# Three edits on one core: a stack loaded from GpSimd's queue, a normalisation moved to GpSimd, and a reordered chain of last reciprocals

## The chip, the cores and the metric

The kernel runs on one core of a Trainium2 chip. The metric is device time in microseconds (us), the median of several executions. Engines are named as the profile names them: PE (matrix multiplication; PEld its weight loads), DVE (vector), ACT (scalar, with the activation functions), POOL (GpSimd) and SP, which here only issues DMAs. ACT and POOL issue DMAs too, each into a queue of its own.

## The reference

For x of 2048 tokens by 640 channels the reference returns a gated sum of an attention block (32 heads of width 20) and a token-mixing MLP:

```python
x = A_x
g = _sigmoid((x * gate_w).sum(-1, keepdims=True))
a = _A_ref(x, A_wqkv, A_wo)                  # softmax(q k^T * Dh**-0.5) v, then @ wo
b = _B_ref(x, B_w1, B_b1, B_w2, B_b2)        # layernorm; u = gelu(w1^T h + b1); y = w2^T u + b2
return g * a + (1 - g) * b
```

All inputs are fp32. The kernel splits most operands into a high and a low part (`hi_lo`, lines 39 to 44) and multiplies them in three passes: high by high, high by low, low by high.

## The kernel before

The kernel runs in stages; times are from the profiled execution.

*Projections (0 to 221 us).* `qk_unit` forms q and k, then the v loop forms v; all go to DRAM. In the last 24 qk units (lines 545 to 576, from 137 us) the first half of x's channels is also loaded (`h_load`), normalised (`h_norm`: subtract the mean, multiply by 1/std) and split (`h_split`: ACT makes the high part `hh`, POOL the low part `hl`). From unit 8 on, the first score stack is loaded as well. A *stack* is the operand of one pair of heads, copied together from DRAM: `ks` (k, three times) and two `qs` halves. With `eng=None` its DMAs are not issued at once but put on a list, `drip`, from which the loops issue one or two at a time.

*MLP with the maximum pass (221 to 738 us).* For each half d of the channels there are 14 u tiles (`u`, layer one) and 16 y tiles (`y`, layer two). The weights are loaded by SP (`w_raw`, line 514), some nine pieces ahead, into 8 buffers, and split by ACT (`wh`) and POOL (`wl`). PE's order comes from a generator, `mlp`, and between its steps the loop at line 798 puts *score* steps: a score matmul `s` (line 210) goes to PSUM, and DVE takes row maxima of it (line 216), or, in pairs, of a score plus the part of another that ACT has cut at zero (lines 225 and 235). The maxima `m` go to DRAM; the attention loop's exponential uses them. How many score steps stand by MLP step n is set by `dve_room(n)`: it gives DVE an even load, of 435 ns for a score step and, in the first half's y tiles, 600 ns for each normalisation of the second half. That normalisation is done there, one tile of 128 tokens in each y tile, by DVE for d = 1 and by POOL for d = 0 (line 483). In this stage the order on ACT, DVE, POOL and SP is also that in which the code emits instructions; a small model of time (`clock`, `act`, `later_on`) decides when each is emitted.

At score step 552 the loop asks for the first *exponential* stack (`st_src[0]`: 20 DMAs), its maxima (`load_m`: eight DMAs of one 4 KB row) and `load_v(0)` (one DMA), all on `drip`; one entry is issued per two score steps, behind what is left of the score stack of that time.

*Attention (738 to 1712 us).* 16 pairs of heads, 32 steps each: two score matmuls into PSUM, exponential on ACT, `pv` with v, and the rest of the score steps. Outputs `o` and row sums `l` go to DRAM; reciprocals of the sums are stored to DRAM, spread over the head's rows (`r_d`).

*Output projection (1712 to 1789 us).* For token tiles t = 1 to 15, PE forms `a` tiles from the first 512 rows of o (called e: `ore` times reciprocals `rbe`, loaded two token tiles at a time by `e_load`) and, from t = 8 on, from the last 128 rows (called l: `orl`, `rbl`) as well. Each `a` tile has a pair of PSUM banks; there are two such pairs. The last four heads' sums come late: `last_load` reads them, `last_recip` inverts them on DVE and stores them to `rc_d`, and `l_rest` loads them back into the last 80 rows of `rbl`, once per head row, four DMAs. The other rows of `orl` and `rbl` are loaded by POOL in `l_load`.

Of the kernel before, what the change touches and what calls it, by code (L numbers as in the profile page):

```python
# [10 lines left out]
OP = mybir.AluOpType  # L11
AX = mybir.AxisListType

P = 128
S, D, H, DH, F = 2048, 640, 32, 20, 1728
NP = H // 2
NT = S // P
NC = D // P
FF = 13
FT = 14  # L20
NDIFF = 8
LAST = 4
# [4 lines left out]
NPAIR = VW * 2  # L27
# [4 lines left out]
def gated_mix(ctx, tc, xT, x, wqk, wv0, wv1, wo, w1, w1t, b1, w2, b2, out):  # L32
    nc = tc.nc
# [30 lines left out]
    rc_d = dram.tile([LAST, S], F32, name="rc_d")  # L64
    r_d = dram.tile([H, DH, S], F32, name="r_d")
    v_d = dram.tile([2, NT, P, 16 * VW], F32, name="v_d")
# [30 lines left out]
    def k8(shape, dt, name):  # L97
        return base.tile(shape, dt, tag="k8", bufs=3, name=name)

    def q4(shape, dt, name):  # L100
        return base.tile(shape, dt, tag="q4", bufs=6, name=name)
# [10 lines left out]
    negm = cp.tile([P, NT], F32, name="negm")  # L112
    ssq = cp.tile([P, NT], F32, name="ssq")
    rstd = cp.tile([P, NT], F32, name="rstd")
# [1 line left out]
    omg = cp.tile([P, NT], F32, name="omg")  # L116
    b2o = cp.tile([P, NT], F32, name="b2o")

    drip = []

    def load_stack(p, ks, qs, full, eng=nc.sync):
        put = eng.dma_start if eng else lambda *a: drip.append(lambda: nc.sync.dma_start(*a))
        for j in range(2):
            r0 = 64 * j
            h = 2 * p + j
            rows = slice(DH * h, DH * h + DH)
            kf = ks.bitcast(F32)
            cut = 0 if full or p >= NDIFF else S if j else S // 2
            for n, lo in enumerate((0, 0, 1)):
                r = slice(r0 + n * DH, r0 + (n + 1) * DH)  # L130
                if cut:
                    put(kf[r, :cut], kd_d[lo, rows, :cut])
                if cut < S:
                    put(kf[r, cut:], k_d[lo, rows, cut:])
            if full:
                put(kf[r0 + 3 * DH: r0 + 3 * DH + 2, :], ones)
            for i in range(2):
                qf = qs[i].bitcast(F32)
                cols = slice(i * (S // 2), (i + 1) * (S // 2))
                put(qf[r0: r0 + DH, :], q_d[0, rows, cols])  # L140
                put(qf[r0 + DH: r0 + 2 * DH, :], q_d[1, rows, cols])
                put(qf[r0 + 2 * DH: r0 + 3 * DH, :], q_d[0, rows, cols])

    def base_stack(p, full, eng=nc.sync):
        ks = k8([P, S], F32R, f"ks{p}_{full}")
        qs = [q4([P, S // 2], F32R, f"qs{p}_{full}_{i}") for i in range(2)]
        load_stack(p, ks, qs, full, eng)
        return ks, qs

    def load_m(p, qs, half, put=nc.sync.dma_start):  # L150
        src = m_d[p, half].rearrange("(g i j t) r -> i j t g r", i=2, j=2, t=8)
        for j in range(2):
            for i in range(2):
                r = 64 * j + 3 * DH + i
                dst = qs[half].bitcast(F32)[r: r + 1, :].rearrange("o (t g r) -> o t g r", g=4, r=32)
                put(dst, src[i: i + 1, j])

    s_src, st_src, v_tiles = {}, {}, {}

    def load_v(p):  # L160
        v_tiles[p] = base.tile([P, NT, NPAIR], F32, tag="v", bufs=2, name=f"v{p}")
        c0 = NPAIR * (p % 8)
        nc.sync.dma_start(v_tiles[p], v_d[p // 8, :, :, c0: c0 + NPAIR].rearrange("t p c -> p t c"))

    s_close = []

    def s_max(p, half, parts):
        mm = cp.tile([P, 16], F32, tag="mm", bufs=2, name=f"mm{p}_{half}")
# [14 lines left out]
    def s_next():  # L183
        next(stream)()
        for e in list(s_close):
            e[0] -= 1
            if e[0] <= 0:
                s_close.remove(e)
                e[1]()
# [242 lines left out]
    for half in range(2):  # L432
        wvh, wvl = wvs[half]
        width = HALF + 2 if half == 0 else HALF
        for t in range(NT):
            n = NT * half + t
# [43 lines left out]

    def h_norm(d, t):
        xm = xms[d, t]
        (nc.vector if d else nc.gpsimd).tensor_scalar(xm, xm, negm[:, t:t + 1], rstd[:, t:t + 1], op0=OP.add, op1=OP.mult)  # L483

    def h_split(d, t):
        xm = xms.pop((d, t))
# [18 lines left out]
    def w_raw(k):  # L505
        src, _ = w_list[k]
        n, m = src.shape[1], src.shape[2]
        if k < AHEAD:
            raw = p1.tile([P, 4, P], F32, tag="xr", bufs=2, name=f"wr{k}")
        elif k < 2 * AHEAD:  # L510
            raw = q4([P, 4, P], F32, f"wr{k}")
        else:
            raw = gp.tile([P, 4, P], F32, tag="wr", bufs=8, name=f"wr{k}")
        (nc.scalar if k < 2 * AHEAD else nc.sync).dma_start(raw[:, :n, :m], src)
        w_raws.append(raw)
# [31 lines left out]
    for n, (m, q) in enumerate(units):  # L547
# [26 lines left out]
        if n == 22:  # L574
            w_split(2)
            w_raw(4)
            w_raw(5)
    xps.close()

    gps = ExitStack()  # L580
    gp = gps.enter_context(tc.tile_pool(name="gp", bufs=1, side="right"))
# [21 lines left out]
    def settle(ns):  # L603
        clock[0] += ns
        for e in sorted(e for e in events if e[0] <= clock[0]):
            events.remove(e)
            e[2]()
        while free[0] <= clock[0] + 100:
            e = min((e for e in act_q if e[1] <= clock[0] + 100), default=None)
            if e is None:  # L610
                break
            act_emit(e)
# [151 lines left out]
    S_AHEAD = NDIFF * 128 + 2 + 48  # L764
    STEPS = 2 * ((FT - 1) * 48 + 32 + NT * 40)
# [4 lines left out]

    hooks[0] = start_ahead
    FIRST = 14
    U_STEPS = (FT - 1) * 48 + 32
    DIFF, RAW, NORM = 435, 640, 600

    def dve_work(k):
        return DIFF * min(k, NDIFF * 128) + RAW * max(0, k - NDIFF * 128)

    def dve_room(n):
        norms = min(max((n - U_STEPS) / (NT * 40), 0), 1) * NT * NORM  # L780
        return (dve_work(S_AHEAD) + NT * NORM) * (n + 1 - FIRST) / (STEPS - 20 - FIRST) - norms

    first_p = {}

    def first_scores(n):
        ks, qs = st_src[0]
        ps = psum.tile([P, 2, 512] if n == 0 else [P, 512], F32, tag=("two", "s3", "pv")[n], bufs=1, name=f"stf{n}")
        pt = k8([P, 512], F32, "pf2") if n == 2 else q4([P, 2, 512] if n == 0 else [P, 512], F32, f"pf{n}")
        todo = ((0, 0, 0), (1, 0, 1)) if n == 0 else ((n - 1, 1, None),)
        for j, c, i in todo:  # L790
            r = slice(64 * j, 64 * j + 3 * DH + 2)
            nc.tensor.matmul(ps if i is None else ps[:, i], ks[r, :P], qs[0][r, c * 512:(c + 1) * 512], start=True, stop=True)
            first_p[j, c] = pt if i is None else pt[:, i]
        nc.scalar.activation(pt, ps, AF.Exp, scale=SCALE)

    steps = mlp(hs)
    done = 0
    for n, _ in enumerate(steps):
        if n == STEPS - 28:
            s_wide[0] = False  # L800
        if n in (STEPS - 22, STEPS - 16, STEPS - 10):
            first_scores((n + 22 - STEPS) // 6)
        settle(146)
        while done + 2 <= S_AHEAD and dve_work(done) < dve_room(n):
            if done == 48:
                s_src[1] = base_stack(1, False, None)
            if done == 4 * 128 + 40:
                st_src[0] = base_stack(0, True, None)
                for half in range(2):
                    load_m(0, st_src[0][1], half, lambda *a: drip.append(lambda: nc.sync.dma_start(*a)))  # L810
                drip.append(lambda: load_v(0))
            if drip:
                drip.pop(0)()
            for _ in range(2):
                s_next()
            done += 2
            settle(233)
# [45 lines left out]
    last_rl = []  # L863
# [6 lines left out]

    def last_recip():
        nc.vector.reciprocal(last_rl[0], last_rl[0])
        nc.sync.dma_start(rc_d.rearrange("h (a b) -> (h a) b", b=LAST * S // P), last_rl[0])

    later = {}

# [97 lines left out]
    def e_low(q, eng=nc.vector):  # L974
        o_low(q, "e", o_hl[q], eng)
# [13 lines left out]
    def l_rest(rb):  # L989
        for h in range(LAST):  # L990
            nc.sync.dma_start(rb[L0 + h * DH:L0 + (h + 1) * DH], rc_d[h:h + 1].broadcast_to([DH, S]))
# [59 lines left out]
    for p in range(NP):  # L1051
# [3 lines left out]
        for it in range(32):  # L1055
            qh, kt = divmod(it, NT)
# [9 lines left out]
            if it == 14 and due_stack:  # L1066
                n = due_stack.pop()
# [63 lines left out]
    last_rb = l_load()  # L1131
    e_high(2, lp)
    for t in range(NT):
        q = t // 2 + 2
        if t % 2 == 0 and 2 < q < NT // 2:
            e_high(q, ap if q % 4 < 2 else lp)
        lates = {NT // 2 - 2: (2, 0), NT // 2 + 1: (3, 1)}.get(t, ())
        evacs = [(t, range(NC) if t >= NT // 2 else range(NC - 1))] if t else []
        if t >= NT // 2:
            evacs.append((t - NT // 2, [NC - 1]))  # L1140
        if t == NT - 1:
            evacs.reverse()
        evacs = [a_tile(*e) for e in evacs]
        for f in evacs:
            f()
        for n in lates:
            l_high(n)
        if t % 2 == 0 and q < NT // 2:
            e_low(q)
            if q + 2 < NT // 2:  # L1150
                e_load(q + 2)
        for n in lates:
            l_low(n)
        if t == 2:
            last_recip()
            l_rest(last_rb)
    ordered.close()
    lps.close()

# [46 lines left out]
```

## Time and profile before

| | us |
|---|---|
| median of three runs | 1792.61 |
| lowest and highest | 1791.98 and 1795.49 |
| the profiled execution | 1791.4 |
| its span, first to last instruction | 1789.5 |
| mean granted TensorE clock | 0.999 |

The page's second part gives the span in 40 slices of 44.7 us, in tenths of a busy engine:

```profile
DVE  5303289899889999776767676676767677767244
ACT  4244388887888887799999999999999999999930
POOL 1113378778877767211111111121322121212200
```

DVE is at eight or nine tenths from slice 6 to slice 16, the MLP; POOL is then at seven or eight tenths; ACT is full in attention. In rows of the windows view each engine has its busy time and, in brackets, its number of instructions; behind them stand the granted clock, the share of the DMA engines and the GB/s moved. In the timeline a row has its start, its duration, the engine, the line and the operation, and in square brackets the engine's idle time before it and what ended that. SPq is SP's queue of DMA issues: a row there has the time of the issue, not of the transfer.

### The profile page before, as it was taken

What the parts mean: (1) busy time and instruction counts of PE and PEld (TensorE: products, weight loads), DVE (VectorE), ACT (ScalarE), POOL (GpSimd) and SP (SyncE); (2) the same over time, 40 slices, a digit from 0 to 9 for tenths busy, and PEclk for the clock granted to TensorE, in tenths of its full rate; (3) what the DMA queues carried; (4) which work ended last, traced back from release to release, by engine and by line L of the source; (5) the groups of instructions that cost most, each with busy time, mean ns of one, the idle gap of its engine ahead of it and who ended that gap; (6) DMA issues with size and microseconds to landing.
All of it is one profiled execution on the core that took longest, in us unless ns stands there. A gap on an engine that the chain in (4) does not pass through costs nothing.

```text
span 1789.5 us, 39923 instructions
## 1 busy us (share of the span) xinstructions
PE 1777.8 (99%) x15000; PEld 1113.8 (62%) x15000; DVE 1236.6 (69%) x2396; ACT 1481.5 (83%) x2534; POOL 632.8 (35%) x887
## 2 busy tenths in 40 slices
PE   9999999999999999999999999999999999999999
PEld 7998899999999999633333333333333333333378
DVE  5303289899889999776767676676767677767244
ACT  4244388887888887799999999999999999999930
POOL 1113378778877767211111111121322121212200
PEclk9999999999999999999999999999999999999999
DMA  8757876556675564335213224043363242301553
GB/s 284 247 172 243 258 194 170 157 158 186 177 188 161 143 186 141 95 59 126 59 28 87 59 57 95 17 100 76 45 140 66 47 93 60 73 13 45 196 137 128
DMA packets 155137, 222.33 MB, mean 124 GB/s; under 512 B 66058, under 2 KB 93082, under 8 KB 151262
## 3 DMA queue, kind: packets, MB, share of 16 engines
q1 hardware_dynamic: 137360, 190.82, 38.5%
q0 software_dynamic: 14848, 23.75, 5.7%
q10 hardware_dynamic: 2736, 5.21, 1.1%
q8 instruction: 118, 1.93, 0.4%
q14 instruction: 75, 0.61, 0.1%
HBM read 165.43 MB, written 53.92 MB: 123 GB/s over the span
## 4 chain that ended last, share of the span: by engine, by line
PE 95%; DVE 3%; DMA 1%; issue 0%; ACT 0%; SPq 0%; DVEq 0%; ACTq 0%
PE pv L911 29%; PE st L1007 21%; PE s L210 12%; PE u L49 11%; PE y L49 8%; PE qk L55 8%; PE v L55 4%; PE a L1116 3%; DVE mx L216 1%; DVE ov L235 1%; DMA rc_d<-rl_last 1%; DVE xm L483 1%; DMA rbl<-rc_d 0%; DMA wr<-in_wqk_dram 0%; DVE oy L1122 0%; PE a L49 0%
## 5 line engine op out<-in xcount | busy, mean ns | idle before, releaser
L216 DVE TENSOR_REDUCE mx<-s 128x1 f32<-128x512 f32 x1280 | 834.7, 686 | 283.1 <-PE s L210 216.4
L1022 ACT ACTIVATE p<-st 128x512 f32<-128x512 f32 x1022 | 582.7, 657 | 0.0
L1014 ACT ACTIVATE p<-st 128x1024 f32<-128x1024 f32 x511 | 551.4, 1079 | 2.2 <-PE s L210 1.6
L911 PE MATMUL pv<-p,v 128*32 128x512 f32 x4088 | 546.8, 605 | 0.0
L1007 PEld LDWEIGHTS st<-qs_True,ks_True 62*128 62x128 f32 x2044 | 244.7, 184 | 430.2 <-ACT p L1014 427.0
L1007 PE MATMUL st<-qs_True,ks_True 62*128 62x512 f32 x2044 | 495.0, 445 | 0.1
L210 PE MATMUL s<-ks_False,qs_False 60*128 60x512 f32 x1152 | 360.8, 395 | 2.2 <-DVE mx L235 1.9
L44 POOL TENSOR_TENSOR wl<-wr,wh 128x512 fp32r<-128x512 f32 x228 | 275.1, 1217 | 79.1 <-ACT wh L41 67.5
L235 DVE CUSTOM_DVE_ANT_0 ov<-s,ov 128x512 f32<-128x512 f32 x384 | 263.7, 687 | 35.2 <-PE s L210 24.2
L225 ACT ACTIVATE ov<-s 128x512 f32<-128x512 f32 x384 | 226.6, 596 | 70.1 <-PE s L210 63.7
L210 PE MATMUL s<-sk,sq 60*128 60x512 f32 x896 | 280.1, 394 | 0.0
L49 PE MATMUL y<-gh,wh 64*128 64x320 f32 x896 | 224.7, 307 | 0.0
L49 PE MATMUL y<-gl,wh 64*128 64x320 f32 x832 | 216.2, 306 | 0.0
L49 PE MATMUL y<-gh,wl 64*128 64x320 f32 x832 | 215.6, 305 | 0.0
L892 POOL DMA_DIRECT2D l_d<-oev x124 | 60.4, 494 | 409.5 <-DVE oev L884 403.7
L210 PEld LDWEIGHTS s<-ks_False,qs_False 60*128 60x128 f32 x1152 | 199.3, 185 | 7.6 <-DVE mx L235 4.7
L49 PE MATMUL u<-hl,wh 64*128 64x320 f32 x864 | 199.0, 307 | 0.0
L49 PE MATMUL u<-hh,wh 64*128 64x320 f32 x864 | 198.8, 307 | 0.0
L911 PEld LDWEIGHTS pv<-p,v 128*32 128x32 f32 x4088 | 82.3, 108 | 175.2 <-issue 162.7
L49 PE MATMUL u<-hh,wl 64*128 64x320 f32 x800 | 187.2, 307 | 0.0
L41 ACT ACTIVATE wh<-wr 128x512 fp32r<-128x512 f32 (+3 forms) x247 | 147.1, 599 | 38.7 <-PE y L49 16.6
L210 PEld LDWEIGHTS s<-sk,sq 60*128 60x128 f32 x896 | 166.0, 185 | 18.5 <-DVE mx L216 0.4
(145 smaller groups left out, 2384.1 us busy)
## 6 DMA issues: line engine op xcount, KB each, us to landing
wr<-in_w_dram SPq DMA_DIRECT2D x192, 256.0 KB
ks_True<-k_d SPq DMA_DIRECT2D x96, 160.0 KB
qs_True<-q_d SPq DMA_DIRECT2D x192, 80.0 KB
qs_False<-q_d SPq DMA_DIRECT2D x108, 80.0 KB
sk<-k_d SPq DMA_DIRECT2D x42, 160.0 KB
sq<-q_d SPq DMA_DIRECT2D x84, 80.0 KB
v_d<-vt SPq DMA_DIRECT2D x32, 168.0 KB
v<-v_d SPq DMA_DIRECT2D x16, 336.0 KB
```

What stands on the lines that cost most here:

```text
L41: nc.scalar.activation(hi, src, AF.Copy)
L44: (lo_eng or nc.vector).tensor_sub(lo, src, hi.bitcast(F32))
L49: nc.tensor.matmul(ps[k], a[r], b[r], start=start, stop=stop)
L55: nc.tensor.matmul(ps, a, b, start=(i == 0 and k == 0), stop=(i == n - 1 and k == 2))
L210: nc.tensor.matmul(ps, qs[half][r, t * P:(t + 1) * P], ks[r, kc * 512:(kc + 1) * 512], start=True, stop=True)
L216: nc.vector.tensor_reduce(mx[:, slot, j, t: t + 1], ps, axis=AX.X, op=OP.max)
L225: nc.scalar.activation(over[j, kc], ps, AF.Relu)
L235: nc.vector.tensor_tensor_reduce(ov, ps, ov, 1.0, -3.0e38, OP.add, OP.max, mx[:, slot, j, t: t + 1])
L911: nc.tensor.matmul(pv[r: r + 32, :], v_tiles[p][:, kt, 10 * j: 10 * j + 32], pt[j, c], start=(kt == 0), stop=(kt == NT - 1))
L1007: nc.tensor.matmul(ps, ks[r, kt * P:(kt + 1) * P], qs[qh][r, c * 512:(c + 1) * 512], start=True, stop=True)
L1014: nc.scalar.activation(pt, ps, AF.Exp, scale=SCALE)
L1022: nc.scalar.activation(pt, ps, AF.Exp, scale=SCALE)
```

## The change

- The first score stack is issued by POOL instead of SP: `drip` asks a variable queue, which is POOL's until the projections' pools are closed, and SP's from then on.
- `h_norm` runs on POOL for both halves; `dve_room` has no term for it any more, so the score steps are spread evenly over all MLP steps.
- From score step 128 on, an entry of `drip` is issued per four score steps instead of two. The first exponential stack, its maxima and v are put on a second list, `slow`, issued in the alternate steps; `load_v(0)` is cut into eight DMAs.
- At the end, `last_recip` stands after tile 1 instead of tile 2, its store is issued by POOL, and `l_rest` stands ahead of `e_load(5)` instead of behind it.

```diff
     def load_stack(p, ks, qs, full, eng=nc.sync):
-        put = eng.dma_start if eng else lambda *a: drip.append(lambda: nc.sync.dma_start(*a))
+        put = eng.dma_start if eng else lambda *a: drip.append(lambda: drip_q[0].dma_start(*a))
...
-    s_close = []
+    s_close, drip_q = [], [nc.gpsimd]
...
-        (nc.vector if d else nc.gpsimd).tensor_scalar(xm, xm, negm[:, t:t + 1], rstd[:, t:t + 1], op0=OP.add, op1=OP.mult)
+        nc.gpsimd.tensor_scalar(xm, xm, negm[:, t:t + 1], rstd[:, t:t + 1], op0=OP.add, op1=OP.mult)
...
     xps.close()
+    drip_q[0] = nc.sync
...
     def dve_room(n):
-        norms = min(max((n - U_STEPS) / (NT * 40), 0), 1) * NT * NORM
-        return (dve_work(S_AHEAD) + NT * NORM) * (n + 1 - FIRST) / (STEPS - 20 - FIRST) - norms
+        return dve_work(S_AHEAD) * (n + 1 - FIRST) / (STEPS - 20 - FIRST)
...
             if done == 4 * 128 + 40:
+                held, drip[:] = list(drip), []
                 st_src[0] = base_stack(0, True, None)
+                put = lambda *a: drip.append(lambda: nc.sync.dma_start(*a))
                 for half in range(2):
-                    load_m(0, st_src[0][1], half, lambda *a: drip.append(lambda: nc.sync.dma_start(*a)))
-                drip.append(lambda: load_v(0))
-            if drip:
+                    load_m(0, st_src[0][1], half, put)
+                load_v(0, 8, put)
+                slow[:], drip[:] = drip, held
+            if drip and (done % 4 == 0 or done < 128):
                 drip.pop(0)()
+            elif slow and done % 4 == 2:
+                slow.pop(0)()
...
         nc.vector.reciprocal(last_rl[0], last_rl[0])
-        nc.sync.dma_start(rc_d.rearrange("h (a b) -> (h a) b", b=LAST * S // P), last_rl[0])
+        nc.gpsimd.dma_start(rc_d.rearrange("h (a b) -> (h a) b", b=LAST * S // P), last_rl[0])
...
             e_low(q)
+            if t == 2:
+                l_rest(last_rb)
             if q + 2 < NT // 2:
                 e_load(q + 2)
         for n in lates:
             l_low(n)
-        if t == 2:
+        if t == 1:
             last_recip()
-            l_rest(last_rb)
```

Order on POOL in the y tiles of the first half, around the end of y tile 8, before (`wl` are weight splits, `ty` the tile's sum, `hl1_8` the low part of the second half's token tile 8):

```order
L700 TENSOR_TENSOR ty0_7_6490<-ty0_7_6490,x2_6523 128x320
L44 TENSOR_TENSOR hl1_7_6551<-xm1_7_6007,hh1_7_6550 128x320
L44 TENSOR_TENSOR wl93_6565<-wr93_6360,wh93_6564 128x512
L44 TENSOR_TENSOR wl94_6601<-wr94_6415,wh94_6600 128x512
L44 TENSOR_TENSOR wl95_6659<-wr95_6469,wh95_6658 128x256
L44 TENSOR_TENSOR wl96_6717<-wr96_6492,wh96_6716 128x512
```

and now:

```order
L703 TENSOR_TENSOR ty0_7_6493<-ty0_7_6493,x2_6514 128x320
L44 TENSOR_TENSOR hl1_7_6548<-xm1_7_6005,hh1_7_6547 128x320
L485 TENSOR_SCALAR xm1_8_6185<-xm1_8_6185,negm_87,rstd_89 128x320
L44 TENSOR_TENSOR wl93_6570<-wr93_6371,wh93_6569 128x512
L44 TENSOR_TENSOR wl94_6606<-wr94_6418,wh94_6605 128x512
L44 TENSOR_TENSOR wl95_6667<-wr95_6470,wh95_6666 128x256
```

The normalisation `xm1_8` now stands between the splits of POOL, one per y tile; from DVE's order the same 16 instructions are gone.

Order on SP in the u tiles of the second half, where the maxima (`m_d`) are loaded among the weights (`wr`), before:

```order
L514 DMA wr139_8522<-in_w1_dram 128x512
L810 DMA qs0_True_0_8057<-m_d_62 1x32x32 x3
L514 DMA wr140_8577<-in_w1_dram 128x512
L810 DMA qs0_True_1_8058<-m_d_62 1x32x32
L514 DMA wr141_8608<-in_w1_dram 128x512
```

and now, some six weight pieces later:

```order
L811 DMA qs0_True_0_7974<-m_d_62 1x32x32
L516 DMA wr146_8850<-in_w1_dram 128x512
L811 DMA qs0_True_0_7974<-m_d_62 1x32x32
L516 DMA wr147_8905<-in_w1_dram 128x512
L811 DMA qs0_True_0_7974<-m_d_62 1x32x32
L122 DMA ks6_False_8890<-kd_d_61 20x1024
L811 DMA qs0_True_0_7974<-m_d_62 1x32x32
L516 DMA wr148_8970<-in_w1_dram 128x512
```

At most one row of maxima now stands between two entries of other kinds; the next score stack (`ks6`) falls into the same stretch.

Order on SP at the end, from the load of the last sums on, before:

```order
L868 DMA rl_last_26472<-l_d_64 128x64
L937 DMA ore4_26485<-o_d_63 128x4x256
L937 DMA rbe4_26486<-r_d_66 128x4x256
L937 DMA ore5_26549<-o_d_63 128x4x256
L937 DMA rbe5_26550<-r_d_66 128x4x256
L873 DMA rc_d_65<-rl_last_26472 128x64
L991 DMA rbl_26477<-rc_d_65 20x2048 x4
L937 DMA ore6_26619<-o_d_63 128x4x256
```

and now:

```order
L874 DMA rl_last_26479<-l_d_64 128x64
L943 DMA ore4_26492<-o_d_63 128x4x256
L943 DMA rbe4_26493<-r_d_66 128x4x256
L997 DMA rbl_26484<-rc_d_65 20x2048 x4
L943 DMA ore5_26562<-o_d_63 128x4x256
L943 DMA rbe5_26563<-r_d_66 128x4x256
L943 DMA ore6_26626<-o_d_63 128x4x256
```

The store to `rc_d` has left SP (on POOL it stands directly behind the loads of `orl` and `rbl`), and the four loads that need it stand ahead of the fifth e load.

More of the change, by code (lines that the diff above doesn't have):

```diff
@@ L117, in gated_mix @@
     b2o = cp.tile([P, NT], F32, name="b2o")
-    drip = []
+    drip, slow = [], []
     def load_stack(p, ks, qs, full, eng=nc.sync):
-        put = eng.dma_start if eng else lambda *a: drip.append(lambda: nc.sync.dma_start(*a))
+        put = eng.dma_start if eng else lambda *a: drip.append(lambda: drip_q[0].dma_start(*a))
         for j in range(2):
@@ L158, in gated_mix, with load_v @@
     s_src, st_src, v_tiles = {}, {}, {}
-    def load_v(p):
+    def load_v(p, pieces=1, put=nc.sync.dma_start):
         v_tiles[p] = base.tile([P, NT, NPAIR], F32, tag="v", bufs=2, name=f"v{p}")
         c0 = NPAIR * (p % 8)
-        nc.sync.dma_start(v_tiles[p], v_d[p // 8, :, :, c0: c0 + NPAIR].rearrange("t p c -> p t c"))
-    s_close = []
+        for i in range(pieces):
+            kt = slice(i * NT // pieces, (i + 1) * NT // pieces)
+            put(v_tiles[p][:, kt], v_d[p // 8, kt, :, c0: c0 + NPAIR].rearrange("t p c -> p t c"))
+    s_close, drip_q = [], [nc.gpsimd]
     def s_max(p, half, parts):
@@ L772, in gated_mix @@
     FIRST = 14
-    U_STEPS = (FT - 1) * 48 + 32
-    DIFF, RAW, NORM = 435, 640, 600
+    DIFF, RAW = 435, 640
     def dve_work(k):
```

## The prediction

> **What bounds the kernel now.** I read the page first, then the windows of each stage, then the waits in the stages where PE does not keep its rate.
>
> ```profile
> span 1789.5 us, 39923 instructions
> PE 1777.8 (99%) x15000; PEld 1113.8 (62%) x15000; DVE 1236.6 (69%) x2396; ACT 1481.5 (83%) x2534; POOL 632.8 (35%) x887
> PE 95%; DVE 3%; DMA 1%; issue 0%; ACT 0%; SPq 0%; DVEq 0%; ACTq 0%
> ```
>
> PE is the bound: 99% busy and 95% of the chain. But a busy PE can be a slow one, so I count matmuls per stretch. In the windows each engine has its busy time and, in brackets, its instructions:
>
> ```profile
> 136.80:220.80 84.00, 84.00 (x363) 67.77 (x361) 24.60 (x38) 31.65 (x58) 28.72 (x35) 1.00 0.80 250
> 390.60:465.60 75.00, 73.13 (x879) 70.55 (x877) 67.85 (x162) 59.48 (x120) 58.68 (x62) 1.00 0.62 181
> 481.00:526.90 45.90, 45.66 (x553) 44.94 (x551) 40.53 (x101) 37.06 (x75) 34.71 (x35) 1.00 0.76 189
> 526.90:565.20 38.30, 38.30 (x471) 38.30 (x470) 34.80 (x91) 32.06 (x65) 31.23 (x35) 1.00 0.68 187
> 613.10:685.00 71.90, 71.90 (x889) 71.67 (x888) 65.27 (x167) 59.29 (x115) 52.64 (x58) 1.00 0.53 159
> 738.50:1711.60 973.10, 973.02 (x7165) 346.29 (x7161) 661.36 (x1068) 970.72 (x1533) 183.90 (x362) 1.00 0.32 74
> 1711.60:1740.00 28.40, 28.40 (x193) 28.16 (x192) 16.62 (x24) 4.25 (x4) 3.09 (x6) 1.00 0.73 183
> 1740.00:1748.10 8.10, 5.30 (x22) 4.48 (x22) 8.10 (x13) 2.29 (x3) 0.00 (x0) 0.79 0.63 217
> 1744.40:1747.80 3.40, 3.40 (x13) 3.09 (x13) 3.40 (x6) 1.06 (x1) 0.00 (x0) 0.50 0.74 263
> ```
>
> Rows 2 and 5 are nine y tiles each, of the first and of the second half of x. The second half starts 889 matmuls in 71.90 us, 80.9 ns each; at that pace 879 would take 71.1 us, not 75.00: **3.9 us lost**. The first half's stretch has 12 score matmuls fewer, which cost more than an average one, so I call it 4.2 (3.9 to 4.5). Rows 3 and 4 are u tiles: 471 in 38.30 is 81.3 ns each, 553 would be 45.0, not 45.90: **0.9 us lost**. Rows 7 and 8 are the tail: 28.40/193 is 147 ns, 22 would be 3.2, not 8.10: **4.9 us lost**, part of it at the granted clock of 0.50. The attention loop has PE and ACT both full, and the change moves nothing there. So about 10 us can be won at all.
>
> **The change part by part. The normalisation of the second half, from DVE to GpSimd.**
>
> ```profile
> PE s L210 <- DVE mx L235: 1.9, 9, 0.3
> L483 POOL TENSOR_SCALAR xm<-xm,negm,rstd x16: 602/608/1177, 148.1 to 208.6; 128x320 f32<-128x320 f32 x16
> L483 DVE TENSOR_SCALAR xm<-xm,negm,rstd x16: 446/1096/1103, 359.6 to 477.1; 128x320 f32<-128x320 f32 x16
> ```
>
> Nine waits of PE for DVE, one per y tile of row 2; each tile's DVE normalisation takes 1.10 us although the planner's table gives it 0.60. The planner thins the score steps for 0.60, DVE falls 0.5 us behind, and a score matmul at the head of PE's queue waits for a PSUM tile. After the change DVE does 16 or 18 score matmuls' reductions per tile, as in row 5, where it keeps up without loss: **-4.2**. The planner now spreads the steps evenly; their number is the same, so that is 0.
>
> On GpSimd this adds one instruction a tile. Row 2 has it busy 58.68/9 = 6.52 us a tile; a tile without stalls takes 71.90/9 = 7.99. With 0.61 (the median of the first half) it is 7.13, with 1.18 (the longest) 7.70: both fit, so the cover is 0.3 to 0.9 us of idle time a tile. If it is gone, the weight splits behind it are late and PE waits for these. I take 0.61, as 16 of them have that median, and 0 for it.
>
> [...]
>
> **Stack and v spread.** While the first exponential stack, eight 4 KB rows of maxima and v are loaded, SP stands between the weight loads:
>
> ```profile
> 512.90 0.38 SPq L514 DMA_DIRECT2D wr<-in_w_dram  x1
> 513.34 2.08 SPq L810 DMA_DIRECT2D qs_True<-m_d  x3
> 515.53 0.38 SPq L514 DMA_DIRECT2D wr<-in_w_dram  x1
> 513.13 0.63 ACT L41 ACTIVATE wh<-wr 128x512 fp32r<-128x512 f32 x1 [0.57 <-DMA wr<-in_w_dram]
> 516.00 0.50 PE L210 MATMUL s<-ks_False,qs_False 60*128 60x512 f32 x2 [0.24 <-ACT ov L225]
> ```
>
> ACT waits for a weight, its copies of scores are late, PE waits for ACT. The change issues one such load per four score steps, but a pending score stack takes the alternate slots, so the density falls only in parts. Of the 0.9 I take **-0.6** (bounds 0 and -0.9). v's DMA becomes eight; SP has them beside weights that are loaded some tiles ahead: 0.
>
> **First score stack by GpSimd.** 21 DMAs leave SP and stand between GpSimd's splits:
>
> ```profile
> L895 POOL DMA_DIRECT2D o_d<-oev x128: 505/512/529, 772.3 to 1714.2; - x128
> 218.57 1.31 POOL L44 TENSOR_TENSOR wtmp<-wr,wtmp 128x512 fp32r<-128x512 f32 x1 [5.20 <-DMA k_d<-evh]
> ```
>
> 21 x 0.51 = 10.7 us, in a stage of 84 us in which GpSimd is busy 28.72 (row 1) and PE never waits. The splits that PE needs first have another 5.2 us of idle time ahead. So **0**; below nothing it cannot go, since row 1 has no PE time to win. Uncovered it would be up to 10.7 late.
>
> **The last reciprocals.** The four last heads' sums go to DRAM and back before l tiles can be formed:
>
> ```profile
> 1721.37 0.36 SPq L937 DMA_DIRECT2D ore<-o_d  x1
> 1721.78 0.92 SPq L937 DMA_DIRECT2D rbe<-r_d  x1
> 1722.75 0.76 SPq L873 DMA_DIRECT2D rc_d<-rl_last  x1
> 1731.97 1.42 SPq L991 DMA_DIRECT2D rbl<-rc_d  x4
> 1733.49 0.39 SPq L937 DMA_DIRECT2D ore<-o_d  x1
> 1717.94 0.56 POOL L982 DMA_DIRECT2D orl<-o_d  x1 [3.23 <-issue]
> 1718.48 0.53 POOL L984 DMA_DIRECT2D rbl<-r_d  x1
> rbl<-r_d POOLq DMA_DIRECT2D x1, 384.0 KB, 10.6
> 1722.75 9.20 DMA rc_d<-rl_last
> 1733.06 6.19 DMA rbl<-rc_d
> 1731.88 1.23 DVE L958 TENSOR_TENSOR ore<-ore,rbe 128x1024 f32<-128x1024 f32 x1 [1.35 <-DMA rbe<-r_d]
> 1733.02 1.00 DVE L1122 SCALAR_TENSOR_TENSOR oy<-a,g_t,oy 128x320 f32<-128x320 f32 x2
> 1739.54 1.29 DVE L958 TENSOR_TENSOR orl<-orl,rbl 128x512 f32<-128x512 f32 x2 [5.52 <-DMA rbl<-rc_d]
> 1744.24 0.70 PE L1116 MATMUL a<-woh,ohl 128*128 128x320 f32 x2 [1.05 <-DVE oy L1122]
> ```
>
> Now: the store took 9.20 us behind 1 MB of e loads in its queue, the loads 6.19; l came at 1739.5, and PE lost the 4.9. After: the reciprocal runs some 3 us earlier, and the store is issued by GpSimd at 1718.48 + 0.53 = 1719.0, in the queue where orl and rbl stand. It could land from 1720.8 (passing them, with the 1.8 us of the fastest store) to 1731.4 (rbl's 1729.1 and 2.3). I take R = 1727: behind rbl, but without the e load that shared the engines. **The new wait:** SP now waits for that landing *before* the fifth e load, which so moves from 1721.4 to R + 1.5 = 1728.5, with the sixth and seventh queued behind. It took 10.1 us to land; behind rbl it takes over 6.2; I take 8.5, hence X = 1737.4 (1735 to 1741). DVE waits for it in order at the ore product, now at 1731.88. By the rows' steps behind X: 1.14 ore, 1.00 oy, 1.21 orl, 1.13 ole, 1.21 oll, 0.92 oy, 1.13 ore, 1.00 oy = 8.7, after which the next tile starts, at 1746.1. The oy of 2.1 us behind X also frees the PSUM for PE's tile of 1736.4: 3.2 us of idle time there, in place of those at 1740. Ten of row 8's matmuls are of the tile that starts at 1746.1; the fifth pair comes at 1747.3, against 1748.1 now: **-0.8**, from +3.0 (X = 1741) to -3.0.
>
> The clock may take some back: after idle time PE ran 3.4 us at half (row 9). If that comes again it falls into the tile behind the 3.2 us, mostly under DVE's 8.7 us chain, so I count 0.2 for it: **-0.6**. [...]
>
> **Sum.** -4.2 - 0.6 - 0.6 = -5.4 against the profiled execution's 1791.4 (its span of 1789.5 and 1.9 around it) is 1786.0. The median of the runs is 1792.6, 1.2 above, so I forecast 1787.0 to 1787.2, and write 1787.0.
>
> **The rivals.**
>
> - *The tail hides all*: R near 1725 and the e load quick; tail -3, spread -0.9, sum -8.2: **1784**, 10%. For it: the store has nothing but reads ahead of it.
> - *The tail gives back*: the store lands at 1729 to 1731 behind orl and rbl. X is 1739.5 to 1741.5, the tail +1.3 to +3.3, the sum -3.5 to -1.5: **1789 to 1791**, 13%. For it: rbl's landing at 1729.1.
> - *The change doesn't do what it says*: GpSimd becomes the bound of the y tiles, the splits come late, and PE waits for these: only the -0.6 and -0.6 are left, **1791.4**, 10%. For it: 89% busy by the sum above; against it: 7.70 of 7.99 even at the worst.
> - *Slower*: SP's new wait at the first rbl load. Each us of R beyond 1727 costs one; with R at 1737 the sum is +4.6, **1797**. It decides against the kernel from R = 1732.4, by 0.2% from 1736. 6%; against it: no landing on that queue in the rows is over 10.6 us.
>
> **How the numbers follow.** The forecast, about 1787, has 61%. A measurement of this kernel can tell about 0.2%, 3.6 us. Faster by that is below 1789.0: 61 + 10 = 71%. Within it: 13 + 10 = 23%. Slower: 6%. The range: the terms' best ends, -4.5, -0.9 and -3.0, give 1784.2, and the 0.6 by which the fastest run lies under the median 1783.5; the other end takes in both "same" rivals up to 1791.0.
>
> **What would show each step.** Right: no PE wait for mx L235 between 390 and 465, the nine tiles at about 80.9 ns a matmul; xm on POOL at 0.61 us; 481 to 527 at 81.3 ns; rc_d landing near 1727 less 5; DVE's wait at ore longer and at orl gone. Wrong: wl releasing PE; PE waiting for wtmp near 220; the tail's 22 matmuls again at 8 us, or an idle PE of over 5 us before them.

## The result and the profile after

| | before | after |
|---|---|---|
| median of 20 executions, us | 1792.27 | 1788.51 |
| lowest and highest | 1789.67 and 1800.57 | 1785.00 and 1793.51 |
| ratio, with its 95% interval | | 0.9980 (0.9973 to 0.9987) |
| the profiled execution | 1791.4 | 1788.71 |
| its span | 1789.5 | 1786.8 |

The change makes the kernel 0.2% faster: 3.6 us, by the interval 2.3 to 4.8. The forecast was 5.4 us and 1787.0.

The page after, its first part and the chain that ended last:

```profile
span 1786.8 us, 39925 instructions
PE 1774.7 (99%) x15000; PEld 1106.2 (62%) x15000; DVE 1227.1 (69%) x2380; ACT 1483.3 (83%) x2534; POOL 654.3 (37%) x925
PE 96%; DMA 3%; DVE 0%; issue 0%; ACT 0%; POOL 0%; SPq 0%; DVEq 0%; ACTq 0%; POOLq 0%
```

In the chain the 3% of DVE are gone and 2 points of DMA have come. The first is DVE's reductions, which hardly stand in it any more. The second is nearly all start-up: by the page's lines the first loads of x and of the weights now have 1% each, and the tail's store has 1% before and after. So the chain doesn't say what was won, and where the time went is read by stage. The windows of each kernel, cut at the first matmul of the MLP, at its last y matmul (by which attention has begun) and at the first matmul behind the last `pv` (projections, MLP, attention, tail), before:

```profile
0.00:220.77 220.77, 218.13 (x1089) 188.33 (x1089) 66.92 (x120) 88.26 (x176) 54.25 (x109) 1.00 0.74 239
220.77:738.22 517.45, 515.23 (x6293) 510.58 (x6294) 464.91 (x1138) 413.70 (x815) 391.61 (x410) 1.00 0.59 165
738.22:1711.61 973.39, 973.31 (x7168) 346.57 (x7165) 661.36 (x1068) 970.72 (x1533) 183.90 (x362) 1.00 0.32 74
1711.61:1789.50 77.89, 71.17 (x457) 68.32 (x456) 43.46 (x70) 8.84 (x10) 3.09 (x6) 0.97 0.50 152
```

and after:

```profile
0.00:221.97 221.97, 218.27 (x1088) 188.44 (x1088) 67.86 (x121) 88.81 (x176) 65.14 (x130) 0.99 0.74 241
221.97:734.17 512.20, 512.09 (x6294) 510.21 (x6294) 454.43 (x1121) 414.84 (x815) 400.84 (x426) 1.00 0.60 165
734.17:1708.14 973.97, 973.54 (x7169) 339.13 (x7165) 661.25 (x1068) 970.80 (x1533) 184.59 (x362) 1.00 0.33 74
1708.14:1786.80 78.66, 70.78 (x457) 68.41 (x456) 43.57 (x70) 8.82 (x10) 3.69 (x7) 0.98 0.48 151
```

The same matmuls in each stage; the lengths (third number of a row) differ by +1.20, **-5.25**, +0.58 and **+0.77** us, together -2.70. The MLP has won more than the whole kernel did.

The +1.20 isn't the change's. It lies in the first 40 us, in which both kernels run the same instructions in the same order. The windows of the first 136 matmuls and of the rest of the projections, before and after:

```profile
0.00:40.00 40.00, 37.36 (x136) 28.44 (x137) 22.78 (x37) 19.75 (x34) 7.01 (x15) 1.00 0.82 278
40.00:220.77 180.77, 180.77 (x955) 159.89 (x953) 44.14 (x84) 68.52 (x142) 47.24 (x94) 1.00 0.73 231
```

```profile
0.00:41.21 41.21, 37.51 (x136) 28.55 (x137) 23.61 (x38) 20.03 (x34) 6.99 (x15) 0.96 0.80 275
41.21:221.97 180.76, 180.76 (x954) 159.89 (x952) 44.24 (x84) 68.78 (x142) 58.15 (x115) 1.00 0.73 233
```

136 matmuls took 40.00 and 41.21 us (granted clock 1.00 and 0.96), the rest 180.77 and 180.76. The MLP begins at 220.77 us before, at 221.97 after, and at 218.89 in the run with the planner's 1100 ns below. This start-up scatter is a part of why single executions spread over 8 us, and it is why the parts below are read by stage.

Two windows answer to the prediction's rows: the nine y tiles of the first half, and the u tiles in which the first exponential stack is loaded:

```profile
391.43:463.04 71.61, 71.61 (x888) 71.34 (x885) 63.91 (x162) 60.80 (x122) 63.74 (x72) 1.00 0.64 188
478.98:523.45 44.47, 44.47 (x548) 44.37 (x545) 39.54 (x102) 36.97 (x75) 33.95 (x35) 1.00 0.78 191
```

71.61/888 is 80.6 ns a matmul (85.3 before), 44.47/548 is 81.1 (83.0 before), and PE is busy throughout both.

### The profile page after: what moved, and what is told of

Read it like the earlier page. It is cut to its first block, busy times and chain, and to the rows that moved or that the text cites. A ratio compares the mean times of both kernels' runs of the same rounds, so it can differ in the third digit from the quotient of the medians.

```text
span 1786.8 us, 39925 instructions
## 1 busy us (share of the span) xinstructions
PE 1774.7 (99%) x15000; PEld 1106.2 (62%) x15000; DVE 1227.1 (69%) x2380; ACT 1483.3 (83%) x2534; POOL 654.3 (37%) x925
## 4 chain that ended last, share of the span: by engine, by line
PE 96%; DMA 3%; DVE 0%; issue 0%; ACT 0%; POOL 0%; SPq 0%; DVEq 0%; ACTq 0%; POOLq 0%
PE pv L917 29%; PE st L1013 20%; PE s L212 13%; PE u L49 10%; PE y L49 10%; PE qk L55 7%; PE v L55 4%; PE a L1122 3%; DMA xr<-in_xT_dram 1%; DMA wr<-in_wqk_dram 1%; DMA rc_d<-rl_last 1%; DMA rbe<-r_d 0%; PE a L49 0%; DMA o_d<-oev 0%; DVE mx L218 0%
## 5 line engine op out<-in xcount | busy, mean ns | idle before, releaser
L1028 ACT ACTIVATE p<-st 128x512 f32<-128x512 f32 x1022 | 567.5, 627 | 0.0
L1020 ACT ACTIVATE p<-st 128x1024 f32<-128x1024 f32 x511 | 536.8, 1051 | 2.6 <-PE s L212 1.8
```

## The experiments

Each part alone was put on the kernel before, or one thing was altered in the changed kernel. A ratio is against the kernel before on the same chip. "Tail" is the time from the first matmul behind the last `pv` to the end of the span.

| run | median us | ratio, interval | MLP | attention | tail |
|---|---|---|---|---|---|
| before | 1792.27 | | 517.5 | 973.4 | 77.9 |
| after | 1788.51 | 0.9980 (0.9973 to 0.9987) | 512.2 | 974.0 | 78.7 |
| normalisation alone | 1789.13 | 0.9982 (0.9971 to 0.9992) | 517.8 | 973.4 | 79.8 |
| planner's 1100 ns alone | 1790.85 | 0.9987 (0.9974 to 1.0000) | 514.6 | 973.6 | 77.4 |
| tail alone | 1794.11 | 1.0009 (0.9996 to 1.0022) | 517.5 | 973.4 | 78.4 |
| spread of loads alone | 1789.92 | 0.9983 (0.9973 to 0.9993) | 519.5 | 973.6 | 77.7 |
| after, store first | 1785.05 | 0.9958 (0.9945 to 0.9970) | 513.2 | 974.0 | 76.0 |
| after, e load first | 1784.96 | 0.9953 (0.9941 to 0.9966) | 512.2 | 973.9 | 74.8 |
| after, both | 1785.52 | 0.9961 (0.9950 to 0.9971) | 512.2 | 974.0 | 76.9 |
| after, store by ACT, e load first | 1783.24 | 0.9954 (0.9939 to 0.9969) | 512.2 | 974.0 | 75.8 |
| after, GpSimd loaded | 1798.55 | 1.0039 (1.0026 to 1.0051) | 523.0 | 974.0 | 79.0 |
| e load first, spread undone | 1786.45 | 0.9965 (0.9953 to 0.9978) | 513.8 | 973.6 | 74.9 |
| after, one queue in order of need | 1785.97 | 0.9964 (0.9952 to 0.9976) | 512.2 | 974.0 | 78.3 |
| after, old tail | 1786.47 | 0.9969 (0.9957 to 0.9981) | 512.2 | 974.1 | 77.1 |

### The normalisation alone

```diff
-        (nc.vector if d else nc.gpsimd).tensor_scalar(xm, xm, negm[:, t:t + 1], rstd[:, t:t + 1], ...)
+        nc.gpsimd.tensor_scalar(xm, xm, negm[:, t:t + 1], rstd[:, t:t + 1], ...)
...
-        return (dve_work(S_AHEAD) + NT * NORM) * (n + 1 - FIRST) / (STEPS - 20 - FIRST) - norms
+        return dve_work(S_AHEAD) * (n + 1 - FIRST) / (STEPS - 20 - FIRST)
```

> The kernel before with the normalisation alone changed: all 16 second-half normalisations on GpSimd, score steps spread evenly; stacks, store and tail as before. Theory (DVE fell 0.5 us per y tile behind because its normalisation took 1.10 us where the planner counts 0.60): the nine waits of PE for mx go, the MLP stage (first u matmul to last y matmul, 517.4 us before, 512.2 after the whole change) becomes 513.2, the u tiles at 510 to 527 us still lose 0.9, the tail stays at 77.9; time -4.2 against before. Rival (the gain of the whole change in these tiles came from the slower drip): 517 and no gain.

By the clock 3.2 us faster (1.4 to 5.2). In its trace no wait of PE for mx is left, and from the start of the MLP to the end of the first half's y tiles it takes 257.0 us, as the changed kernel does, against 260.2 before (with more score matmuls in them than before, so that the gain is larger than the difference). But the u tiles behind, 548 matmuls, took 50.14 us in this execution:

```profile
477.24:527.38 50.14, 47.60 (x548) 45.91 (x546) 39.89 (x103) 36.93 (x75) 33.94 (x36) 0.97 0.73 180
```

against 44.47 in the changed kernel, so that its MLP shows no gain. The waits in 488 to 530 us of this kernel:

```profile
PE s L210 <- ACT ov L225: 2.5, 3, 2.0
ACT wh L41 <- DMA wr<-in_w1t_dram: 3.2, 2, 2.9
```

It is the stall that the prediction costed at 0.9, with the same order of events (a weight late behind stack loads, ACT late, PE late), six times as long.

### A true due time instead

```diff
-    DIFF, RAW, NORM = 435, 640, 600
+    DIFF, RAW, NORM = 435, 640, 1100
```

> The kernel before with one number changed: the planner counts 1100 ns instead of 600 for each second-half normalisation, which stays on DVE. Theory (a wrong due time, not DVE's total load, made PE wait): about one score step in sixteen of a y tile moves elsewhere, most of the nine waits go, and the MLP stage is 513 to 514.5, time -3 to -4. Rival 1 (DVE has too much work with the normalisation wherever the steps stand, or the normalisation itself holds up the score steps for 1.1 us longer than the PSUM tiles can bridge): the stage keeps 516 to 517.4. Rival 2: the moved steps make the u tiles DVE-bound, and the same 4 us are lost there.

The MLP took 514.55 us, 2.9 less than before, and the list of PE's waits has no mx any more, though DVE still does all 16 normalisations. By the clock it is 2.3 us faster (0 to 4.7), less than the 3 to 4 that were expected. So PE waited because the planner gave DVE too little time for them, not because DVE had too much to do. The move to GpSimd cures the same thing; it isn't the only cure.

### The tail alone

```diff
         nc.vector.reciprocal(last_rl[0], last_rl[0])
-        nc.sync.dma_start(rc_d..., last_rl[0])
+        nc.gpsimd.dma_start(rc_d..., last_rl[0])
...
+            if t == 2:
+                l_rest(last_rb)
             if q + 2 < NT // 2:
                 e_load(q + 2)
...
-        if t == 2:
+        if t == 1:
             last_recip()
-            l_rest(last_rb)
```

> The kernel before with the tail alone changed (reciprocals after tile 1, their store from GpSimd's queue, the four reciprocal loads ahead of the fifth e load). Theory (the profile after: SP waits 10.2 us for the store, the fifth e load starts 8 us late and PE stands idle 4.0 us before tile 8 instead): MLP as before, 517.4; the tail 78.7 instead of 77.9, time +0.8 against before. Rival (the tail's loss after comes from the different phase in which this execution reached it): the tail within 77 to 77.9 or better.

Time +1.6 us (interval -0.7 to +3.9, so unclear by itself); tail 78.4, MLP as before. PE's only wait in the tail is the one of the profile after:

```profile
PE a L1116 <- DVE oy L1122: 3.9, 1, 3.9
```

### The spread of the loads alone

```diff
-            if drip:
+            if drip and (done % 4 == 0 or done < 128):
                 drip.pop(0)()
+            elif slow and done % 4 == 2:
+                slow.pop(0)()
```

(with the second list and v in eight pieces, as in the change)

> The kernel before with the loads alone spread (one per four score steps, first exponential stack and v on the second list, v in eight pieces). Theory: the u tiles of 510 to 527 us lose nothing instead of 0.95 us, the nine waits in the first half's y tiles stay (4.2 us), MLP stage 516.5, time -0.9 or less. Rival (the stall at 510 to 527 followed from DVE being late out of the y tiles): it stays, 517.4, no gain.

By the clock 3.0 us faster (1.3 to 4.8), more than either theory allowed. Its profiled execution, 552 matmuls in the u tiles, shows the opposite:

```profile
481.09:528.96 47.87, 45.86 (x552) 44.95 (x550) 40.44 (x101) 37.28 (x75) 34.75 (x35) 1.00 0.80 174
```

At 81.1 ns these would take 44.8: 3.1 us lost, with the spread in place. This execution and that of the normalisation alone were 3.4 and 4.3 us slower than their medians. With 0.9 us before, 5.7 with the normalisation alone and 3.1 here, the stall isn't a fixed cost but one that differs from execution to execution, and one profile can't size it.

### The store ahead of the loads

```diff
-    last_rb = l_load()
     e_high(2, lp)
...
         if t == 1:
             last_recip()
+            last_rb = l_load()
```

> The changed kernel with one order changed: the store of the last reciprocals stands ahead of GpSimd's loads of orl and rbl instead of behind them. Theory (the store took 9.5 us because it was queued behind 1.4 MB of reads in the same queue): it lands some 2.5 us after its issue, at about 1718 by the times of the profile after, SP's wait ahead of the fifth e load is about 1 us instead of 10.2, that load lands at about 1729 instead of 1735, PE is not idle before tile 8, and the tail takes 73 to 74.5 instead of 78.7; time 4 to 5.5 below the changed kernel. Rival (the DMA engines are full at that time whatever the queue, so that a store of 256-byte pieces takes 6 to 9 us anyway): SP's wait stays over 6 us and the tail over 76.

The chain of waits of this kernel has, as in the changed kernel, the store and then the e load (start, us):

```profile
1714.35 3.58 DMA rc_d<-rl_last
1719.84 12.13 DMA rbe<-r_d
```

The store takes 3.58 us instead of 9.54: it was late because of the loads ahead of it. SP's wait falls to 4.2 us, and the fifth e load goes out 12.1 us into the tail instead of 18.0. But that load's second half (`rbe`) now takes 12.1 us instead of 8.5; orl and rbl (issued at 1715.05 and 1715.59 us, 6.4 and 7.9 us to land) are in flight with it, and the four reciprocal loads were issued in the 1.9 us ahead of it. PE waits 2.0 us, the tail is 76.0: half of what was expected.

### The fifth e load first

```diff
-            if t == 2:
-                l_rest(last_rb)
             if q + 2 < NT // 2:
                 e_load(q + 2)
+            if t == 2:
+                l_rest(last_rb)
```

> The changed kernel with one order changed back: the four reciprocal loads stand behind the fifth e load on SP; the store stays on GpSimd's queue behind orl and rbl. Theory (the loss after is the fifth e load's delay): it is issued at about 1718, PE is not idle before tile 8, the store lands at about 1725, the reciprocal loads at 1731 to 1733, in time for DVE; the tail takes 73 to 74.5. Rival (the four loads then queue behind 1 MB of e loads and land after 1735): PE waits for the l tiles again as in the kernel before, tail 75 to 78.

The tail is 74.8 us, 3.9 less than after and a little over what was expected (DVE still waits 1.6 us for the reciprocal loads), and the time is 0.9953 of before (0.9941 to 0.9966), which lies wholly below the changed kernel's interval: with this one order put back the kernel beats both. The store was as slow as before (10.3 us), yet that costs nothing here, because only the reciprocal loads stand behind it. So the new tail's loss is the position of one wait in SP's order.

### Both, and the store by ACT

```diff
-        nc.gpsimd.dma_start(rc_d..., last_rl[0])
+        nc.scalar.dma_start(rc_d..., last_rl[0])
```

(the second one; with the e load first, and orl and rbl ahead as in the change)

> Both orders: the store ahead of orl and rbl, the reciprocal loads behind the fifth e load. Theory: no PE wait in the tail, 73 us, the clock granted in full; time about 5.5 below the changed kernel, 1783. Rival (orl and rbl, now later, take the place of the awaited load): tail over 75.

> As the kernel with the fifth e load first, but the store is issued by ACT's queue, in which nothing else stands. By the queue theory it lands 2 to 3 us after its issue, the tail is 73 to 74.5. By the rival (engines full) it lands after 6 to 9 us, as on GpSimd's queue, and the tail equals that of the kernel with the fifth e load first.

The two edits together gave a tail of 76.9, worse than the e load first alone. From its chain of waits:

```profile
1714.08 4.10 DMA rc_d<-rl_last
1719.49 14.57 DMA rbl<-rc_d
```

The store lands early, the reciprocal loads go out 6.2 us earlier in the tail than with the e load first, and then take 14.6 us instead of 6.9. With ACT's queue, in which nothing else stood, the store took as long as on GpSimd's:

```profile
1713.25 9.15 DMA rc_d<-rl_last
```

That refutes the queue theory as I had stated it: not its place in a queue delays the store, but `orl` and `rbl`, the 1.4 MB issued ahead of it, from whichever queue it goes. It isn't all bulk ahead that does this: the fourth e load, 1 MB, was issued by SP 1.2 to 1.6 us ahead of the store also where the store took 3.6 to 4.1 us. In the run with ACT's queue `rbl`, issued by GpSimd 0.4 us ahead of the store, took 9.4 us, which puts its landing at 1722.2; the store landed at 1722.4. In the changed kernel the two landed at 1724.5 and 1724.7, with the e load first at 1722.7 and 1722.9. So an own queue gave the store no precedence here. Why it landed just behind `rbl` in these three is not shown.

### GpSimd loaded until it doesn't fit

```diff
         nc.gpsimd.tensor_scalar(xm, xm, negm[:, t:t + 1], rstd[:, t:t + 1], ...)
+        for _ in range(3 * d):
+            nc.gpsimd.tensor_scalar(xm, xm, 0.0, 1.0, ...)
```

> The changed kernel with GpSimd's work in the y tiles of the first half raised: behind each of the 16 moved normalisations it adds zero and multiplies by one on the same tile three times more (0.61 us each, 1.84 us a tile; the result is unchanged). In the profile after GpSimd is busy 63.74 us in nine such tiles of 71.61, 7.08 of 7.96 us each, and its weight splits stand 3 to 6 us ahead of PE. Theory (the moved instruction was free because it lay within 0.9 us of idle time): with 8.92 us a tile it does not fit, 0.96 us a tile is missing, 15 us in 16 tiles, of which the 3 to 6 us of lead are spent first; the y stage takes 136 to 140 us instead of 127.3 and PE waits there for weight splits; time +9 to +12. Rival (GpSimd has more room than its busy time shows, since waits stretch its instructions): y stage below 130.

The y tiles of the first half, of the changed kernel and of this one, and this one's waits there:

```profile
351.66:478.98 127.32, 127.32 (x1575) 126.91 (x1573) 113.69 (x287) 108.09 (x216) 112.88 (x127) 1.00 0.64 183
```

```profile
350.45:487.02 136.57, 132.36 (x1576) 128.13 (x1573) 113.80 (x287) 108.82 (x217) 129.65 (x169) 0.99 0.57 166
```

```profile
DVE mt L180 <- POOL mc L44: 5.5, 3, 3.6
PE s L212 <- DVE mx L237: 2.9, 2, 2.5
PE y L49 <- POOL wl L44: 1.1, 2, 0.6
```

The stage takes 9.2 us more, the kernel 10.0, with GpSimd busy for 129.65 us of 136.57: its cover is real and ends about where its busy time says. The added instructions took 0.46 us each, not 0.61:

```profile
L487 POOL TENSOR_SCALAR xm<-xm x48: 458/460/466, 359.9 to 488.9; 128x320 f32<-128x320 f32 x48
```

So the expected 9 to 12 us came out partly by luck: with 0.46 the same sum gives 7.08 + 1.38 = 8.46 us a tile of 7.96, 8 us too much in 16 tiles, and 2 to 5 once the lead of 3 to 6 us is spent. The price isn't paid only where I had put it: of the waits behind GpSimd the longest is that of DVE, whose transposition of maxima (`mt`) stands in order behind GpSimd's `mc`, so that its reductions are held up and PE waits for mx.

### The spread undone in the best version

```diff
-            if drip and (done % 4 == 0 or done < 128):
+            if drip:
                 drip.pop(0)()
-            elif slow and done % 4 == 2:
-                slow.pop(0)()
```

> The kernel with the fifth e load first (median 1784.96, 0.9953 of before), with the spread of the stack and v loads undone: one entry per two score steps, v in one piece, as in the kernel before. Theory 1 (the spread is worth what the one profile of before showed, 0.6 to 0.9 us): 1785.6 to 1786, and the u tiles at 480 to 525 us lose 1 us. Theory 2 (the stall there varies from one execution to the next, 1.0 us in two profiles without the spread and over 5 in a third, and the spread removes 2 to 3 us in the mean): 1787 to 1788, 0.997 of before. Rival (the spread does nothing on average; a profile with it also showed 3.0): 1785.

0.9965 against 0.9953, 2.1 us by the ratios and 1.5 by the medians. That lies between the two theories, and the intervals overlap, so that the rival isn't excluded by the clock alone. Its u tiles took 45.68 us for 548 matmuls, 1.2 more than after:

```profile
479.78:525.46 45.68, 45.14 (x548) 44.40 (x546) 39.82 (x103) 37.12 (x76) 34.02 (x36) 1.00 0.78 194
```

Over the runs, the loss in these tiles against 81.1 ns a matmul was 0.5 to 1.2 us in four profiles without the spread and 5.7 in the fifth; with it, 0 in six, 1.1 in one and 3.1 in one (that with GpSimd loaded left out). The means are 1.9 and 0.5, but the 5.7 makes most of this difference: without it the first is 1.0.

### All loads of the tail in one queue

```diff
-        nc.gpsimd.dma_start(raw..., o_d[r0:])
+        nc.sync.dma_start(raw..., o_d[r0:])
...
             if q + 2 < NT // 2:
                 e_load(q + 2)
+            if t == 2:
+                l_rest(l_load())
```

(rbl likewise)

> The changed kernel with all loads of the tail in one queue, in the order in which they are needed: SP issues the fourth and fifth e load, then orl and rbl (GpSimd's until now), then the four reciprocal loads, then the sixth e load; the store of the reciprocals stays on GpSimd's queue, now with no loads ahead. Theory (what is left in the tail of the kernel with the fifth e load first, 2.2 us, comes from the e loads sharing the DMA engines with 1.4 MB of orl and rbl that are not needed until 20 us later): the fourth e load lands within 6 us, DVE does not wait for it, the tail is 72.7 to 73.5 us, and the time 1.5 to 2 us below that kernel, 1783. Rival (orl and rbl, some 5 us later now, are late themselves, and DVE waits at the l product): tail 75 to 78.

The fourth e load is in time and DVE doesn't wait for it, as expected; but the four reciprocal loads, issued from 1717.4 us on, arrive at 1732.4:

```profile
1718.77 13.65 DMA rbl<-rc_d
```

DVE waits 5.1 us for them, and the tail is 78.3: the rival, by another load than the one it named. Issued in the order of need, they still didn't arrive in time. The sixth e load, issued at 1721.6 us, was in flight beside them; how much of the 13.7 us it cost was not tried.

### The old tail in the changed kernel

> The changed kernel with its tail undone: the last reciprocals after tile 2, their store on SP's queue behind the fifth e load, the four reciprocal loads behind it. Theory (the new tail costs about as much as the profiles say: 78.64, 78.43 and 78.95 us with it; 77.92, 77.35, 77.67 and once 79.84 with the old one, 0.5 in the mean): tail near 78, the time 0.5 below the changed kernel, 1788. Rival 1 (the new tail costs more than its profiles show; the tail alone was timed 1.6 us slower): 1787. Rival 2 (the old tail is the slower one in most executions, as the 79.84 was): 1789.5 or more.

(The tail's three edits taken back.) Time 0.9969 of before, 2.0 us below the changed kernel, with overlapping intervals; tail 77.1. This is nearest to rival 1. Eight profiles: 77.1, 77.4, 77.7, 77.9 and 79.8 with the old tail, 78.4, 78.7 and 79.0 with the new. By profiles the new tail costs 0.7 us in the mean, by the two timed comparisons 1.6 and 2.0; all three have the same sign, but none is clear of the scatter (the old tail of 79.8 is longer than every new one), and the size stays open.

## Why the prediction was right, and where it was not

The time, 1788.5, lies in the range and the direction is right; the forecast's sum of -5.4 came out as -3.6 by the clock. Leaving out the start-up, the profile gives -5.25 + 0.58 + 0.77 = -3.9.

**The normalisation (-4.2): right, for the reason given.** The nine waits are gone, the tiles run at 80.6 ns where 80.9 were foreseen. GpSimd takes 0.612 us for each (median of all 32), as taken, and PE never waits for it. That the due time of 0.60 was the cause is shown by the run that corrected only this number.

```profile
L485 POOL TENSOR_SCALAR xm<-xm,negm,rstd x32: 602/612/1152, 149.3 to 476.2; 128x320 f32<-128x320 f32 x32
```

**The stack by GpSimd (0): right.** 180.77 us became 180.76, while GpSimd's busy time there rose by 58.15 - 47.24 = 10.9 us (10.7 foreseen).

**The spread (-0.6): the mechanism right, the size open, its bound of 0.9 too narrow by the clock.** The profile of before lost about 1 us in these tiles, like three of the four others without the spread; the fourth lost 5.7. In the MLP stage as a whole the normalisation and the spread together brought 5.25, not 4.8; timed alone the spread brought 3.0 (1.3 to 4.8), in the best version 2.1. The one profile of the spread alone had a stall of 3.1 us, so no profile shows where its 3.0 us by the clock come from.

**The tail (-0.6): the sign was wrong.** The step that failed is R, the landing of the store, taken as 1727 "behind rbl, but without the e load that shared the engines". The rows of the changed kernel (chain of waits, then timeline):

```profile
1715.14 9.54 DMA rc_d<-rl_last
...
1726.58 8.53 DMA rbe<-r_d
```

```profile
1724.69 1.42 SPq L997 DMA_DIRECT2D rbl<-rc_d  x4
1726.15 0.39 SPq L943 DMA_DIRECT2D ore<-o_d  x1
...
1735.20 1.23 DVE L964 TENSOR_TENSOR ore<-ore,rbe 128x1024 f32<-128x1024 f32 x1 [8.15 <-DMA rbe<-r_d]
...
1737.03 1.00 PE L1122 MATMUL a<-woh,ohe 128*128 128x320 f32 x2 [4.00 <-DVE oy L1128]
...
1744.02 0.65 PE L1122 MATMUL a<-woh,ohe 128*128 128x320 f32 x2
```

This tail begins 3.47 us earlier than the one of before, so the prediction's times less 3.47 stand beside these:

| step | predicted | measured |
|---|---|---|
| store issued | 1715.5 | 1715.14 |
| R, store landed | 1723.5 | 1724.68 |
| fifth e load issued | 1725.0 | 1726.15 |
| X, DVE's ore product | 1733.9 | 1735.20 |
| PE idle ahead of the tile | 3.2 us | 4.0 us |
| next tile, X + 8.7 | 1742.6 | 1744.02 |

Every step is as described. The store took 9.54 us instead of 8.0; it was issued 0.4 earlier, so R was 1.2 late, and that went through to X and to the next tile, one for one, as the price in the "slower" rival said. What came lies between the forecast and the rival in which the tail gives back (+1.3 to +3.3). With 0.2 us more in that tile's first pairs, -0.8 became +0.77. The e load itself was sized right (8.53 us from the issue of its second half, 8.5 foreseen). That the store stood behind 1.4 MB of loads, and not the e load, decided its time is shown by putting it ahead of them: 3.58 us.

The half clock did come, as the row of before had made me count it:

```profile
1737.00:1740.30 3.30, 3.27 (x12) 3.16 (x13) 3.30 (x6) 1.83 (x3) 0.00 (x0) 0.51 0.10 34
```

It lies under DVE's chain: 1735.20 + 8.7 is 1743.9, where the next tile starts. So it can't have cost much more than the 0.2 counted for it. Here it came behind 4.0 us of idle time; two other runs show a lower clock behind shorter waits. With the normalisation alone PE waited 2.0 us in one piece, up to 506.7 us. Its matmuls took 0.31 us until 507.7, as ahead of the wait, but the mean granted clock was 0.95 in 490 to 510 us and 0.96 in 510 to 530, between windows of 1.00. With GpSimd loaded PE waited 2.5 us, up to 412.8: the mean clock of 408 to 420 us was 0.86, and the y matmuls that started from 414.4 to 417.0 took 0.47 us each, against 0.31 from 417.4 on.

Two side sums of the prediction are off, without weight for the forecast: -4.2 - 0.9 - 3.0 is -8.1, not -8.2, and X = 1741 gives +2.8, not +3.0.

**Attention, which the prediction put at nothing:** it took 0.58 us more, and 973.9 to 974.1 in every run that holds both the normalisation and the spread, against 973.4 to 973.6 without one of them. 0.4 of it is a wait at its entry:

```profile
PE st L1013 <- DVE ty L697: 0.4, 1, 0.4
```

Why that wait is longer was not tried.

## What to carry to other kernels

A planner's due time that is half of what the instruction takes (here 0.60 and 1.10 us) showed as a small wait repeated once per tile (nine of at most 0.3 us); correcting the number alone brought 2.9 us of the stage, where the moved work and the spread together brought 5.25. Where the wait was moved ahead of other issues on SP's queue, the transfers behind it paid for it (the fifth e load went out some 8 us later in the tail): leave it behind whatever is needed sooner. And the stall where these transfers met had no fixed size, from 0 to 5.7 us in the profiles, so take several profiles before giving it a price, and a range of several times the one seen.

## What the hardware showed beyond that

- A 32 KB store took 3.6 to 4.1 us issued ahead of the loads of `orl` and `rbl` (1.4 MB) and 8.1 to 10.3 us behind them, and 9.15 us behind them in a queue of its own: a separate queue didn't make it pass.
- The four reciprocal loads of 160 KB took 6.2 us in the kernel before, 6.6 with the old tail, 6.9 with the e load first and 9.1 with the store by ACT, but 13.7 and 14.6 us when they were issued 5 to 6 us earlier than with the e load first, beside the other loads: the whole lead was lost again, and they landed 1.6 to 1.9 us later in the tail.
- GpSimd's tensor_scalar on 128x320 took 0.61 us with two columns of scalars and 0.46 us with two constants.
- PE idle for 4.0 us in one piece was followed by a granted clock of 0.51 for 3.3 us, and idle for 2.5 us by a mean of 0.86 over the 12 us around it. Idle for 1.6 us in one piece (the store first) it kept 1.00, yet in the kernel before three waits of 0.9, 0.8 and 1.1 us between 1740.0 and 1744.2 us were followed by 0.50 for 3.4 us. So in these runs the length of the longest wait doesn't tell whether a half clock follows.
